# Local attention and two feed-forward layers on one core: scalings on GpSimd, padded V, one copy of the second transpose bank, and a new start

## The chip, the cores and the metric

The kernel runs on one core of a Trainium2 chip. A core has five engines with their own instruction streams: PE (TensorE, matrix products), DVE (VectorE), ACT (ScalarE), POOL (GpSimd) and SP, which here only starts DMA transfers; they wait for each other by semaphores. PE, DVE and ACT reach the eight PSUM banks; POOL works on SBUF only. The metric is the device time of one execution in microseconds (us).

## The reference

Attention with a window and a few global keys, then two feed-forward layers; batch 2, 8 heads, 768 positions, head size 64, all in float32:

```python
scores = scale * np.matmul(q, k.transpose(0, 1, 3, 2))
rel = pos[:, None] - pos[None, :]; is_global = pos[None, :] < 8; is_local = (rel >= 0) & (rel < 96)
keep = is_global | is_local
dist = np.where(is_global & ~is_local, 96.0, np.abs(rel))
bias = -slopes[:, None, None] * dist[None, :, :]
scores = np.where(keep, scores + bias[None], -1e9)
a = np.exp(scores - np.max(scores, axis=-1, keepdims=True))
a = a / (np.sum(a, axis=-1, keepdims=True) + 1e-09)
x = np.matmul(a, v)                # -> 1536 tokens x 512
h = x @ w_in;  g = np.where(h > 0, h, np.exp(np.minimum(h, 0)) - 1);  x = g @ w_out
h = x @ w_in2; g = h / (1 + np.exp(-1.702 * h));                      x = g @ w_out2
```

The weights (512x2048 and 2048x512) come as float64 and are converted on the chip.

## The kernel before

**Attention** goes by rows of 128 queries: 12 rows, each in two units of two head pairs, 24 units `u`. A unit of a row that isn't the first of its batch sees 192 keys for each half of the queries; in a first row (units 0, 1, 12, 13) 64 and 128. A unit does, in this order:
- scores on four 64x64 quarters of the array (L330);
- for each of its four blocks `n` a DVE reduce that adds the distance bias and finds the extreme (L639) and an ACT exponential with its sum (L643). The bias is a product of distances and the head's slope: for first rows made per unit by `slope` (`E<-d,slope`: DVE L245 or ACT L553), for others once in `dist` (`d<-gt,slope`);
- 1e-9 and reciprocal (L646, L649), then four scalings of the weights by the reciprocal (`o_ts`, DVE, L245);
- PE transposes into bank `ta` (L661, L664) and bank `tb` (L668, L670);
- copies of the banks to `pt` (`evac`, L677, ACT or DVE). The keys of the two query halves overlap in `tb`: rows 0 to 63 are needed with V's own block, rows 64 to 127 with the block before it (`va`). They are copied apart to `pt[0:64, 0:256]` and `pt[64:128, 768:1024]`, whose other halves `Band` filled with zeros on POOL (L543, L544), so that a product over all 128 rows is right;
- P times V (L700) on two halves of the array, 64 columns of weights each, and, each second unit, `xh` and `xl`, the two parts of the result for the layers (L716, L719).

A float32 matmul stands as two instructions in the trace. `E` has three buffers, `pt` two.

**The layers** run as products of high and low parts (three matmuls for one): `A` (L432, first product, with its activation, L441 to L450), `B` (L472, second product, L489, L493). Weights are converted by `conv`, eight tiles of 128x512 for a group: DMA to `raw`, a scaled copy to `m` (L399 on ACT or L400 on DVE), L402, L404 and L406 on DVE's integer path, then high part (L233, L234) and low part (L240).

**The order** of all this within the branch `banded` is made by `Plan`, a list scheduler that runs while the program is written: each node has a due time, one or more engines it can go to with a cost for each, and keys that it reads and writes. An engine takes, among the nodes that could start soonest, the one due first; a node with several engines goes where its end, plus `BIAS` (DVE 1.373, ACT 0.264, POOL 0), is soonest. `START` says when each engine is free, `TIMES` the distance of the units' due times, `CONV0` that of the first conversions. If PE would wait early in the kernel, the plan puts fillers on it (L732), products of zeros into a free bank, to keep its clock up.

**The start** (`start`, before the branch): the loads, six warm-up matmuls (L282), distances `rel` on POOL and DVE, the scores of row 0, then from the two integers `n_global` and `n_local` (`n_raw`) on DVE a flag (L288 to L295) that says whether the banded form holds, the scaled window (L296, L297) and `d0`, the distances of a first row (L300, L301, twice each). Every engine loads the flag and branches.

## Time and profile before

| what | us |
|---|---|
| median of 3 runs | 613.66 |
| lowest, highest | 613.49, 614.02 |
| the profiled execution | 613.83 |
| its span, first to last instruction | 612.0 |
| PE busy | 599.4 |
| DVE busy | 403.8 |
| ACT busy | 316.3 |
| POOL busy | 4.6 |

Times in rows are microseconds from the span's start unless marked ns. A busy engine had at least one instruction under way; matmuls overlap, so the pace of a run of them is read from start to start. `PEld` is PE's loading of weights. `PEclk` is the granted clock of PE, 1.00 for 2.4 GHz and 0.50 for 1.2 GHz.

### The profile page before, as it was taken

Reading aid. Unit: us, or ns where it says so; the run is one execution under the profiler, and the core shown is the slowest. Engines: PE = TensorE matmul, PEld = TensorE weight load, DVE = VectorE, ACT = ScalarE, POOL = GpSimd, SP = SyncE. Lnnn points to the kernel's source line nnn. Section 1 sums busy time; section 2 is a strip of 40 time slices with the busy share of each in tenths; the row PEclk is TensorE's granted clock in tenths of the full one; section 3 lists DMA queues with packets and bytes.
Section 4 is the critical chain, followed back from the end, with each engine's and each line's share of the span. In section 5 each row is a group of like instructions: output and inputs, shape, how many; then the busy total and the mean of one; then the engine's idle time right before and its main releaser. Section 6 shows DMA issues by size and latency. Waiting matters only on the chain.

```text
span 612.0 us, 8793 instructions
## 1 busy us (share of the span) xinstructions
PE 599.4 (98%) x3332; PEld 494.3 (81%) x3332; DVE 403.8 (66%) x926; ACT 316.3 (52%) x700; POOL 4.6 (1%) x34
## 2 busy tenths in 40 slices
PE   8988999999999999999999999999999999999996
PEld 5777887788888888888888888888888888888885
DVE  7999898539853994489747973388438853753432
ACT  5999889658552562265456553454214522521320
POOL 3000000000000000000000000000000000000000
PEclk9989999999999999999999999999999999999999
DMA  7755565002220331013201330043002320001012
GB/s 262 256 174 190 191 198 189 29 1 101 92 83 1 103 130 43 1 70 131 77 1 35 103 137 1 1 137 126 13 2 103 104 69 1 35 1 69 18 52 74
DMA packets 16467, 52.04 MB, mean 85 GB/s; under 512 B 1952, under 2 KB 2208, under 8 KB 16416
## 3 DMA queue, kind: packets, MB, share of 16 engines
q1 hardware_dynamic: 16128, 50.73, 24.0%
q10 hardware_dynamic: 288, 0.66, 0.3%
q8 instruction: 28, 0.46, 0.3%
q14 instruction: 23, 0.19, 0.1%
HBM read 48.24 MB, written 3.15 MB: 84 GB/s over the span
## 4 chain that ended last, share of the span: by engine, by line
PE 92%; ACT 3%; DVE 3%; DMA 1%; issue 0%; DVEq 0%; ACTq 0%
PE bank L432 43%; PE bank L472 42%; PE bank L700 3%; PE bank L330 2%; PE bank L664 1%; ACT E L643 1%; ACT pt L677 1%; DVE E L639 1%; DVE E L245 1%; DMA n_raw<-in_ns_dram 1%; PE bank L670 0%; ACT m L399 0%; ACT xh L716 0%; ACT E L553 0%; DVE xl L719 0%
## 5 line engine op out<-in xcount | busy, mean ns | idle before, releaser
L432 PE MATMUL bank<-xh,wbig 128*128 128x512 f32 (+1 forms) x560 | 173.6, 381 | 2.5 <-DVE xl L719 1.8
L432 PEld LDWEIGHTS bank<-xh,wbig 128*128 128x128 f32 x560 | 104.4, 189 | 24.3 <-DVE xl L719 2.6
L432 PE MATMUL bank<-xl,wbig 128*128 128x512 f32 (+1 forms) x280 | 105.8, 378 | 0.0
L472 PE MATMUL bank<-g,wbig 128*128 128x512 f32 (+1 forms) x360 | 81.5, 368 | 0.4 <-DVE xl L719 0.2
L432 PE MATMUL bank<-xh,kT 128*128 128x512 f32 x240 | 77.6, 391 | 0.0
L472 PEld LDWEIGHTS bank<-g,wbig 128*128 128x128 f32 x360 | 62.5, 188 | 12.6 <-issue 1.0
L493 DVE SCALAR_TENSOR_TENSOR acc<-bank,acc 128x512 f32<-128x512 f32 x48 | 33.2, 692 | 50.0 <-PE bank L472 49.6
L448 ACT ACTIVATE e<-bank 128x512 f32<-128x512 f32 x48 | 28.6, 596 | 68.0 <-PE bank L432 67.9
L432 PEld LDWEIGHTS bank<-xl,wbig 128*128 128x128 f32 x280 | 53.0, 189 | 9.5
L472 PE MATMUL bank<-wbig,g 128*128 128x512 f32 (+1 forms) x246 | 59.8, 384 | 0.0
L240 DVE TENSOR_TENSOR g<-gt,g 128x512 fp32r<-128x512 f32 (+1 forms) x70 | 46.4, 663 | 19.8 <-ACT g L233 18.6
L233 ACT ACTIVATE wbig<-m 128x512 fp32r<-128x512 f32 x43 | 27.0, 628 | 60.7 <-PE bank L432 39.8
L233 ACT ACTIVATE g<-gt 128x512 fp32r<-128x512 f32 (+1 forms) x70 | 42.6, 608 | 24.0 <-DVE gt L450 15.0
L450 DVE SCALAR_TENSOR_TENSOR gt<-e,bank 128x512 f32<-128x512 f32 x48 | 32.9, 686 | 31.1 <-ACT e L448 30.7
L432 PEld LDWEIGHTS bank<-xh,kT 128*128 128x128 f32 x240 | 45.0, 188 | 9.9 <-issue 0.6
L472 PEld LDWEIGHTS bank<-wbig,g 128*128 128x128 f32 x246 | 45.4, 188 | 9.1
L445 DVE SCALAR_TENSOR_TENSOR gt<-e,bank 128x512 f32<-128x512 f32 (+1 forms) x52 | 33.3, 644 | 21.1 <-ACT e L443 20.6
L432 PE MATMUL bank<-xl,kT 128*128 128x512 f32 x120 | 46.7, 389 | 0.0
L399 ACT ACTIVATE m<-raw 128x512 f32<-128x512 f32 x56 | 37.2, 664 | 15.0 <-DMA raw<-in_w2i_dram 5.9
L404 DVE SCALAR_TENSOR_TENSOR raw<-raw 128x512 int32<-128x512 int32 x64 | 44.1, 689 | 0.8
L406 DVE SCALAR_TENSOR_TENSOR m<-m,raw 128x512 int32<-128x512 int32 x64 | 44.0, 688 | 0.8
L643 ACT ACTIVATE E<-E,st 128x192 f32<-128x192 f32 (+1 forms) x96 | 41.2, 431 | 3.8 <-DVE st L639 3.7
(122 smaller groups left out, 847.0 us busy)
## 6 DMA issues: line engine op xcount, KB each, us to landing
raw<-in_w1i_dram SPq DMA_DIRECT2D x16, 512.0 KB, 3.3
raw<-in_w1o_dram SPq DMA_DIRECT2D x16, 512.0 KB, 3.3
raw<-in_w2i_dram SPq DMA_DIRECT2D x16, 512.0 KB, 3.2
raw<-in_w2o_dram SPq DMA_DIRECT2D x16, 512.0 KB, 3.3
row<-in_qk_dram SPq DMA_DIRECT2D x8, 768.0 KB, 6.4
v<-in_v_dram SPq DMA_DIRECT2D x12, 256.0 KB, 3.5
va<-in_v_dram SPq DMA_DIRECT2D x10, 256.0 KB, 3.8
out_dram<-acc SPq DMA_DIRECT2D x8, 256.0 KB, 2.0
```

The source lines that it names most:

```text
L233: ("ACT", n / 1200 + (0.05 if psum else 0.09), lambda: nc.scalar.activation(out, in_, AF.Copy)),
L240: return [("DVE", n / 960 + 0.068, lambda: nc.vector.tensor_tensor(out, a, b, ALU.subtract))]
L399: ("ACT", 0.52, lambda: nc.scalar.activation(mf, topf, AF.Copy, scale=sc)),
L404: node(due + 1, [("DVE", 0.6, lambda: V.scalar_tensor_tensor(top, bot, 29, top, ALU.logical_shift_right, ALU.bitwise_or))], [kr], [kr])
L406: node(due + 1.5, [("DVE", 0.6, lambda: V.scalar_tensor_tensor(m, m, 3, top, ALU.logical_shift_left, ALU.bitwise_or))], [km, kr], [km])
L432: nc.tensor.matmul(h(), lhsT=w[:, kk, :], rhs=x[:, kk, :], start=(kk == 0 and j == 0), stop=(kk == KK - 1 and j == 2))
L445: node(due + 1, [("DVE", n / 960 + 0.07, lambda: V.scalar_tensor_tensor(gt, e, -1.0, h(), ALU.add, ALU.max))], [ke, b], [kg], uses=[b])
L448: node(due, [("ACT", n / 1200 + 0.05, lambda: S.activation(e, h(), AF.Tanh, scale=0.851))], [b], [ke], uses=[b])
L450: node(due + 1, [("DVE", n / 960 + 0.07, lambda: V.scalar_tensor_tensor(gt, e, 1.0, h(), ALU.add, ALU.mult))], [ke, b], [kg], uses=[b])
L472: nc.tensor.matmul(o(), lhsT=lhsT, rhs=rhs, start=(f == 0 and j == 0), stop=(f == GF - 1 and j == 2))
L493: node(due, [("DVE", n / 960 + 0.07, lambda: V.scalar_tensor_tensor(acc, o(), sc, acc, ALU.mult, ALU.add))], [b] + ka, ka, uses=[b])
L643: node(at + 0.5, [("ACT", W / 1200 + 0.28, lambda n=n, e=e: nc.scalar.activation(e, e, AF.Exp, bias=st[:, n:n + 1], scale=-1.0, accum_out= ...
```

## The change

- The scalings of the weights by the reciprocal, and the products with the slope, get POOL as a further choice in the plan (`o_scale` in place of `o_ts`).
- `tb` is copied once, whole, to `pt[:, 512:768]`; `pt` loses its zero halves. Instead V is padded: `vz` (V's rows 0 to 63, zeros below) and `vaz` (zeros, and `va`'s rows 64 to 127), made by a POOL copy of 64x512 for each load of V and of `va`. One half of the queries uses `vz` with `va`, the other `v` with `vaz`, so P times V becomes twice as many matmuls of 64 columns instead of 128. In first rows the second transposes take all 128 columns; `E`'s columns 192 to 255 are set to zero at the start.
- At the start: `n_raw` is loaded on ACT's queue instead of SP's, row 0's halves change queues, row 1 comes in one transfer on SP; the flag's chain has one dependent step less (an extra instruction for negative integers moves to the general branch); `d0` is made by two instructions over 192 columns from a copy of the distances (`own`).
- The plan: new start times, due times, first conversions and costs; PE's nodes carry a `mode`, the tiling of the array they use, and a node of another mode counts as 0.1 us later and as due 2 us later; transposes keep the order of the units.

```diff
-CONV0 = (-12.46, 4.78)
+CONV0 = (-12.46, 4.0)
-TIMES = (8.0, 4.0, 3.25)
+TIMES = (7.0, 3.0, 2.6)
-START = dict(PE=5.8, ACT=5.1, DVE=5.9, POOL=5.9, SP=5.6)
+START = dict(PE=5.3, ACT=5.0, DVE=5.2, POOL=6.3, SP=5.0)
-ROW0 = 5.2, 5.8
+ROW0 = 4.9, 5.8
+DRAIN = 0.1
+KEEP = 2.0
+RESERVE = 1000.0
...
+                if e == "PE":
+                    wait = min((x[1] for x in ts if x[0] >= 1e9), default=1e9) + RESERVE
+                    ts = [(1e9 if lst[i].alloc and due > wait else t + DRAIN * (
+                        lst[i].mode != self.mode), due + KEEP * (lst[i].mode != self.mode), i)
+                        for t, due, i in ts]
...
-def o_ts(k, out, in_, s1, s2, op0, op1, n):
-    nc = k.nc
-    return [("DVE", n / 1920 + 0.068, lambda: nc.vector.tensor_scalar(out, in_, s1, s2, op0, op1))]
+def o_scale(k, out, in_, c, n):
+
+    op = lambda e: lambda: e.tensor_scalar(out, in_, c, 1.0, ALU.mult, ALU.mult)
+    return [("DVE", n / 1940 + 0.13, op(k.nc.vector)), ("POOL", n / 760 + 0.268, op(k.nc.gpsimd))]
...
-    nc.sync.dma_start(out=raw, in_=ns.bitcast(I32).partition_broadcast(128))
+    nc.scalar.dma_start(out=raw, in_=ns.bitcast(I32).partition_broadcast(128))
     load()
...
+    for e in k.E:
+        G.memset(e[:, :, QW:256], 0.0)
...
+    for (x, n), at in zip(OWN, (128, 2 * QW - 128)):
+        V.tensor_copy(own[:, x:x + n], rel[:, at:at + n])
...
-    V.scalar_tensor_tensor(neg, lo, 0.0, hi, ALU.is_lt, ALU.add)
-    V.scalar_tensor_tensor(n, neg, float(2.0 ** 32), lo, ALU.mult, ALU.add)
-    k.ng, k.nl = n[:, 0:1], n[:, 1:2]
-    V.scalar_tensor_tensor(a, n, 1.0, lim, ALU.mult, ALU.is_le)
-    V.scalar_tensor_tensor(c, k.nl, 1.0, a[:, 1:2], ALU.is_ge, ALU.mult)
-    V.tensor_tensor(flag, c, a[:, 0:1], ALU.mult)
+    V.scalar_tensor_tensor(k.n, k.f[:, 1:4:2], float(2.0 ** 32), k.f[:, 0:4:2], ALU.mult, ALU.add)
+    k.ng, k.nl = k.n[:, 0:1], k.n[:, 1:2]
+    V.scalar_tensor_tensor(a, k.n, 1.0, lim, ALU.mult, ALU.is_le)
+    for x in range(2):
+        V.scalar_tensor_tensor(c[:, x:x + 1], k.n[:, x:x + 1], float(x), a[:, x:x + 1], ALU.is_ge,
+                               ALU.mult)
+    V.tensor_tensor(flag, c[:, 0:1], c[:, 1:2], ALU.mult)
...
-    for x, n, (d, _) in ((128, 64, OWN[0]), (2 * QW - 128, 128, OWN[1])):
-        at, to = rel[:, x:x + n], k.d0[:, d:d + n]
-        V.scalar_tensor_tensor(w[:, 0:n], at, k.ns, k.big[:, 0:n], ALU.is_ge, ALU.mult)
-        V.scalar_tensor_tensor(to, at, k.ns, w[:, 0:n], ALU.min, ALU.add)
+    V.scalar_tensor_tensor(w, own, k.ns, k.big, ALU.is_ge, ALU.mult)
+    V.scalar_tensor_tensor(k.d0, own, k.ns, w, ALU.min, ALU.add)
...
-        self.pt = [t([128, 1024], F32, f"pt{i}") for i in range(2)]
-        for pt in self.pt:
-            k.nc.gpsimd.memset(pt[64:128, 0:256], 0.0)
-            k.nc.gpsimd.memset(pt[0:64, 768:1024], 0.0)
+        self.pt = [t([128, 768], F32, f"pt{i}") for i in range(2)]
+        self.vz = [t([128, H, D], F32, "vz"), k.d[:, :, QW:256]]
+        self.vaz = [t([128, H, D], F32, "vaz")] * 2
...
+        for kind, z, v, rows in (("v", self.vz[p], self.v[p], slice(0, 64)),
+                                 ("va", self.vaz[p], self.va[p], slice(64, 128))):
+            if kind == "v" or r % NB:
+                node(due + 11, [("POOL", 0.63, lambda z=z, v=v, rows=rows: k.nc.gpsimd.tensor_copy(
+                    z[rows], v[rows]))], [(kind, p)], [self.kz[kind][p]])
...
-            evac(due + 3, pt[:, 256:768], lambda: ta.tile, ta, kp[1], 512)
-            evac(due + 3.3, pt[64:128, 768:1024], lambda: tb.tile[64:128, 0:256], tb, kp[2], 256)
-        evac(due + 3.2, pt[0:64, 0:256], lambda: tb.tile[0:64, 0:256], tb, kp[0], 256)
+            evac(due + 3, pt[:, 0:512], lambda: ta.tile, ta, kp[0], 512)
+        evac(due + 3.2, pt[:, 512:768], lambda: tb.tile[:, 0:256], tb, kp[1], 256)
...
             for j, pr in enumerate(prs):
...
+                for x in range(2):
+                    ws = ((self.v if x else self.vz)[p], (self.vaz if x else self.va)[p])
+                    at = (2 * j + 1, 4 + j) if x else (4 + j, 2 * j)
+                    for own in range(first, 2):
+                        for hd in range(2):
+                            o, c = pr * 128 + 64 * x, 128 * at[1 - own] + 64 * (hd ^ x)
+                            nc.tensor.matmul(
+                                xb.tile[64 * hd:64 * hd + 64, o:o + 64],
+                                lhsT=ws[1 - own][:, 2 * pr + hd, :], rhs=pt[:, c:c + 64],
+                                start=(own == first), stop=(own == 1))
...
-        for r in range(2):
-            load_row(r, (nc.scalar, nc.sync))
+        load_row(0, (nc.sync, nc.scalar))
+        load_row(1)
         load_v(0, k.v[0])
```

## Rows read from the trace of the kernel before

**Rows 1.** Table by stretch: us, busy time (instructions) by engine, clock, DMA.
```profile
8.00:67.00 59.00, 54.30 (x584) 44.47 (x583) 55.65 (x243) 57.04 (x192) 0.36 (x2) 0.97 0.61 211
67.00:606.60 539.60, 539.60 (x2714) 446.36 (x2713) 343.01 (x666) 257.46 (x506) 0.00 (x0) 1.00 0.20 70
```

**Rows 2.** Chain that ended last: start us, us, what.
```profile
6.10 0.16 DVE n_flag L295
6.55 0.30 DVE e L300
...
7.58 0.36 DVE d L301
...
8.45 0.22 DVE E L639
...
145.08 10.88 PE bank L472 x48
```

**Rows 3.** PE's timeline, then L732 by stretch, PE and PEld.
```profile
22.36 1.67 PE L732 MATMUL bank<-q1h 128*128 128x256 f32 x12
...
8.00:14.30 6.30, 3.60 (x22) 3.02 (x22) 1.00 0.87 325
...
8.00:67.00 59.00, 7.32 (x42) 5.73 (x42) 0.97 0.61 211
```

**Rows 4.** PE's waits in 8 to 67 us; table by stretch.
```profile
PE bank L432 <- DVE xl L719: 1.8, 1, 1.8
...
37.70:41.10 3.40, 3.40 (x22) 3.07 (x17) 3.28 (x16) 3.29 (x10) 0.00 (x0) 0.50 0.47 162
```

**Rows 5.** Busy time by stretch of L245 (DVE), then of L553 (ACT).
```profile
8.00:67.00 59.00, 14.70 (x60) 0.97 0.61 211
...
8.00:67.00 59.00, 4.87 (x15) 0.97 0.61 211
```

**Rows 6.** Groups by form, 8 to 67 us: xcount, busy us, mean ns, idle.
```profile
L677 ACT ACTIVATE pt<-bank 64x256 f32<-64x256 f32 x23 | 8.6, 373 | 0.2
...
L677 ACT ACTIVATE pt<-bank 128x512 f32<-128x512 f32 x10 | 5.9, 591 | 0.4 <-PE bank L670 0.3
...
L404 DVE SCALAR_TENSOR_TENSOR raw<-raw 128x512 int32<-128x512 int32 x8 | 5.5, 691 | 0.1
...
L240 DVE TENSOR_TENSOR wbig<-m,wbig 128x512 fp32r<-128x512 f32 x7 | 4.8, 690 | 0.2
...
L402 DVE TENSOR_SCALAR raw<-raw 128x512 int32<-128x512 int32 x8 | 3.4, 427 | 0.3 <-ACT m L399 0.3
```

**Rows 7.** Table by stretch, 40 to 70 us.
```profile
40.00:70.00 30.00, 28.41 (x280) 23.90 (x279) 27.19 (x99) 27.90 (x88) 0.00 (x0) 0.98 0.51 169
```

**Rows 8.** POOL's timeline.
```profile
4.60 0.29 POOL masks.py:199 TENSOR_SCALAR_AFFINE_SELECT ident<-ident 128x128 f32<-128x128 f32 x1
...
7.39 0.30 POOL L544 MEMSET pt<- 64x256 f32 x1
```

**Rows 9.** DVE's timeline: the cast that waits for `n_raw`.
```profile
5.04 0.17 DVE L288 CAST n_f<-n_raw 128x4 f32<-128x4 int32 x1 [1.88 <-DMA n_raw<-in_ns_dram]
```

**Rows 10.** PE's timeline; groups by form from 70.25 to 70.5 us.
```profile
43.45 0.44 PE L700 MATMUL bank<-pt,va 128*64 128x128 f32 x4
...
44.48 0.88 PE L330 MATMUL bank<-row 64*64 64x192 f32 x16
...
L330 PE MATMUL bank<-row 64*64 64x64 f32 x8 | 0.4, 230 | 0.0
```

**Rows 11.** Timelines of DVE and POOL at the start.
```profile
1.70 0.47 DVE L277 TENSOR_SCALAR e<-e,n_off 128x384 f32<-128x384 f32 x1 [0.28 <-POOL e L265]
2.01 0.19 POOL L274 MEMSET slope<- 64x1 f32 x1
2.60 0.56 DVE L279 TENSOR_TENSOR e<-e,gt 128x384 f32<-128x384 f32 x1
2.65 0.09 POOL L274 MEMSET slope<- 64x1 f32 x1
```

More of the change, by code (lines that the diff above doesn't have):

```diff
@@ L66 @@
 class Node:
[L67 removed]
+    __slots__ = ("due", "opts", "npred", "succ", "ready", "alloc", "uses", "spare", "mode")
 ENGINES = ("PE", "ACT", "DVE", "POOL", "SP")
@@ L98, in __init__, with node @@
         self.cand = {e: [] for e in self.avail}
-    def node(self, due, opts, reads=(), writes=(), alloc=None, uses=(), spare=2):
+        self.mode = "full"
+    def node(self, due, opts, reads=(), writes=(), alloc=None, uses=(), spare=2, mode="full"):
         n = Node()
+        n.mode = mode
         alloc = [] if alloc is None else alloc if isinstance(alloc, list) else [alloc]
@@ L206, in place @@
         cost = opt[1]
+        if e == "PE" and self.mode != n.mode:
+            t, self.mode = max(t, self.avail[e] + DRAIN), n.mode
         if e == "PE" and t < WARM:
@@ L608, in unit @@
         pt = self.pt[u % 2]
-        kp = [("pt", u % 2, x) for x in range(3)]
+        kp = [("pt", u % 2, x) for x in range(2)]
         V = nc.vector
@@ L623, in unit @@
             halves = range(2) if whole else (half,)
-            node(due, [("PE", 0.25 + (0.23 if first else 0.335) * len(ps), lambda: scores(
-                k, r, ps, [b.tile for b in own]))], self.keys(r, halves), own, alloc=own, uses=own)
+            node(due, [("PE", (0.22 if first else 0.33) * len(ps), lambda: scores(
+                k, r, ps, [b.tile for b in own]))], self.keys(r, halves), own, alloc=own, uses=own,
+                mode="quarters")
         sc = self.sc[2 * half:2 * half + 2] if whole else self.sc
@@ L632, in unit @@
                     d, kd = e, (kE, n)
-                    self.slope(due + 0.1 * n, e, self.d0[:, OWN[x][0]:OWN[x][0] + W], 2 * pr + x, W,
+                    self.slope(due + 0.1 * n, e, self.d0[:, OWN[x][0]:sum(OWN[x])], 2 * pr + x, W,
                                ["d0"], [(kE, n)])
@@ L692, in pv @@
         def pv():
-            blocks = pt.rearrange("p (a b) -> p a b", b=64)
             for j, pr in enumerate(prs):
-                for own in range(first, 2):
-                    v = self.v[p] if own else self.va[p]
-                    for hd in range(2):
-                        a, b = ((2 * j, 6 + 4 * j) if own else (4 + 4 * j, 12 + 2 * j))
-                        a, b = a + hd, b + 1 - hd
-                        nc.tensor.matmul(
-                            xb.tile[64 * hd:64 * hd + 64, pr * 128:(pr + 1) * 128],
-                            lhsT=v[:, 2 * pr + hd, :], rhs=blocks[:, a:b + 1:b - a, :],
-                            start=(own == first), stop=(own == 1))
-        kv = [("v", p)] + ([] if first else [("va", p)])
-        node(due + 4, [("PE", 0.65 if first else 1.1, pv)], kv + kp, [xb],
-             alloc=xb if half == 0 else None, uses=[xb], spare=0)
+                for x in range(2):
[8 more added lines that the diff above has]
+                                start=(own == first), stop=(own == 1))
+        kv = [y for x in ("v", "va")[:2 - first] for y in ((x, p), self.kz[x][p])]
+        node(due + 4, [("PE", 0.5 if first else 0.95, pv)], kv + kp, [xb],
+             alloc=xb if half == 0 else None, uses=[xb], spare=0, mode="columns")
         if half == 0:
```

61 lines of the change are left out of this document (31 added, 30 removed).

## The prediction

> **What bounds the kernel now.** I read the table of busy time by stretch first, then the chain that ended last, then the groups and single instructions of the stretch that the change touches. By stretch [rows 1] the kernel has three parts. From 67 us to 606.6 us TensorE (PE) is busy without a gap at the full granted clock; after it come 5.4 us, to the span's end, of last sums and stores. From 8 to 67 us PE is busy 54.30 of 59 us, while VectorE (DVE) is busy 55.65 and ScalarE (ACT) 57.04: here these two are the limit. GpSimd (POOL) works 0.36 us in that stretch. The chain [rows 2] says the same: it runs through DVE's start instructions until the first `tensor_tensor_reduce` at 8.45 us, then through DVE and ACT, and later, as in its last row shown, through PE alone. So the kernel ends 5.4 us after PE has done its whole work, and a saving is either time that PE wastes before 67 us, or work of PE itself.
>
> What PE wastes in 8 to 67 us has three terms. It isn't busy for 59 - 54.30 = 4.70 us [rows 1]. It runs 42 filler matmuls (L732), which serve only to keep it busy; twelve in a row took 1.67 us [rows 3], 0.139 us each, so 42 take 5.8 us. And one stretch of 3.40 us ran at a granted clock of 0.50, half speed, after PE had waited 1.8 us for `xl` [rows 4]: 1.7 us lost. The sum is 12.2 us, so PE's own work in the stretch is 59 - 12.2 = 46.8 us. That is all that faster DVE and ACT can give there. Of it, 22 fillers (3.1 us) stand before 14.3 us [rows 3], while the first units pass through their chain; more throughput doesn't remove them.
>
> **The change, part by part.**
>
> *The scalings on POOL.* DVE's scalings (L245) take 14.70 us busy in the stretch, 60 of them; ACT's products with the slope (L553) 4.87 us [rows 5]. The planner now has POOL as a third choice for both, with no bias against it, where DVE's end is counted 1.373 us later; I take it that nearly all go there.
>
> *One copy instead of two.* A unit of a row that isn't first copied `tb` twice, 64x256 each, and now once, 128x256. Each such unit makes one copy of 128x512, and the stretch has 10 of them; at 0.373 us a 64x256 copy [rows 6] this takes 3.7 us from ACT. That a copy over 128 partitions costs as much as one over 64 I take from the 128x512 one, 0.591 us: twice the columns and twice the partitions for 1.6 times the price.
>
> *What this gives.* DVE and ACT held 55.65 + 57.04 = 112.7 us. Less 14.70, 4.87 and 3.7 leaves 89.4 us, 44.7 each if the planner spreads what both can do (weight copies, evacuations), and at today's busy share, 112.7/118 = 95.5%, 46.8 us. PE's own work was 46.8 us too. So after the change all three engines would be near their limit together, and then none is always busy: in 40 to 70 us, where today all three come nearest to that, DVE and ACT were busy 27.19 and 27.90 and PE 28.41 of 30 us [rows 7], 5.3% idle. I take 5.3% of a stage of some 48 us, 2.5 us, and the first 3.1 us of fillers as left: 5.6 us wasted instead of 12.2, a gain of **6.6 us**. Bounds: 0 and 12.2 us.
>
> *POOL's own load.* No row has a POOL multiplication by a column of scalars. The nearest are the 128x128 affine select, 0.29 us, and the 64x256 memset, 0.30 us [rows 8]. For 128x192 I take 0.45 us: half as wide again as the select gives 0.44. From below it is 0.29, from above twice the 0.44, 0.88. 60 of them are 27 us. The zero-padded copies are new work on POOL: one 64x512 for each unit, at most twice that memset; I take 0.55 us, for some 13 units 7 us. 34 us together fits in a stage of 48. At 0.88 us it would be 60 us, but the planner then hands what comes late back to DVE. In the chain of a unit, four scalings of 0.45 us, 1.8 us, stand for four that took 14.70/60 each, 1.0 us, on DVE [rows 5]: 0.8 us later, which three `E` buffers carry while PE has other units and FFN work. With that cover gone it would be 0.8 us once for each unit that PE waits for. A copy of V waits for V's load and has the same cover.
>
> *The start.* The flag's chain has five steps after the cast today, the last of them at 6.10 us [rows 2], 1.06 us after the cast's start at 5.04 us [rows 9]: 0.2 us each. Now it has four, and a fifth that waits for nothing new and costs what it takes to issue, some 0.08 us: -0.12 us. Four instructions make `d0`, 6.55 to 7.93 us, 1.38 us [rows 2]. Two over 192 columns replace them; on the chain a 64-wide one takes 0.30 and a 128-wide one 0.36, so 0.42 each, 0.84 in all: -0.5 us. Both lie on the chain to 8.45 us: **-0.6 us**; bounds 0 and -1.1 (POOL's branch and ACT's slopes may still be what the first unit waits for). At nothing I cost: DVE's two copies into `own`, in its wait for `n_raw` (1.88 us idle [rows 9]), 0.7 us if that were gone; POOL's three memsets of `E`, at most 0.9 us by the 64x256 row, between its last start instruction, over at 4.89 us [rows 8], and the flag at 6.1; the order of the loads (`n_raw` is first on ACT's queue as it was on SP's, row 0's second half is behind it, row 1 is whole on SP, and PE has fillers until it is there). POOL's memsets in the branch grow from 4 x 0.30 to 3 x 0.55 us; POOL starts work some 0.4 us later, and ACT and DVE can make the first slopes until then. Were `n_raw` late, everything in the branch would be late by the same.
>
> *PE's own work.* P times V goes from 16 instructions of 128 columns to 32 of 64 for a unit (8 to 16 in a first row's). The columns are the same. Today the 16 take 1.03 us, from 43.45 to 44.48 [rows 10]. Below, nothing is added; above, each 64-column instruction costs what one of 128 does. No row has 64 columns on half the array, but 8 score instructions of 64 columns started on two quarters within 0.25 us beside four wider ones [rows 10], about 0.06 us for each on its quarter. Sixteen on each half at 0.058 are 0.93 us, against 8 at 0.109, 0.87: +0.06 us for 20 units, **+1.3 us** with the first rows'. Against it the planner now charges 0.1 us for a change of the array's tiling and prefers to stay in one. A P times V of 1.03 us holds 0.87 us of columns, so its two edges cost 0.16; if half a change is saved for each of 24 units, that is **-1.0 us** (bounds 0 and -2). All of this lies where PE never waits, so it counts in full: +0.3 us together.
>
> **The sum.** The profiled execution took 613.83 us, 0.2 above the median of 613.66 and 1.8 above its span. 613.83 - 6.6 - 0.6 + 0.3 = **606.9 us**.
>
> **The rivals.**
>
> *POOL and DVE take turns.* POOL's 64x1 memset of 2.01 us took 0.19 us instead of 0.09 and ended 0.03 us after the DVE `tensor_scalar` beside it, that of 1.70 us [rows 11]. So some DVE instructions hold POOL up. If the weight conversion's instructions do so too, POOL's 34 us and DVE's L402, L404, L406 (like L404) and `wbig` L240 (3.4 + 5.5 + 5.5 + 4.8 = 19.2 us [rows 6]) follow one another: 53 us, at 95.5% 55.7 us, and the stage gives back 3.3 us at most; with waits in the units' chain, 2. The time would be about **611.5 us**. Against it: a memset beside the two-input `tensor_tensor` of 2.60 us took 0.09 us [rows 11], but a memset reads nothing. The Trainium skill ("SBUF — State Buffer", the section on the shared port pair) has this as a rule: an exclusive lock, taken by DVE's two-port modes and, against a POOL instruction that reads, by DVE instructions with two SBUF inputs. By that rule the time is this rival's; by the memset row alone it is the forecast's. The first half of the rule agrees with the 0.19 us; the second half no row here shows.
>
> *All waste goes.* If the new order lets PE fill every gap, first fillers included: 613.83 - 12.2 - 0.6 + 0.3 = **601.3 us**. For it: the load of DVE and ACT falls by a fifth. Against: all three engines meet the same 46.8 us.
>
> *Weight loads bound P times V (slower).* If every one of the 32 instructions, whose weights change each time, takes 0.0545 us of the array as today's 16 do, a unit takes 1.89 instead of 1.03 us: 20 x 0.87 + 4 x 0.44 = 19 us, **625 us**. It outweighs the rest from 0.35 us a unit, that is from 38 ns an instruction against 27 by columns. Against it stands the row of 64-column scores.
>
> *Nothing moves, or the new order stumbles.* If the planner's new due times start units that then wait for POOL, waits move rather than go; PE's wait of 1.8 us and its half-clock stretch are what one such place costs, 3.5 us: two of them cancel the gain, 614 us.
>
> **Chances.** Forecast 0.57 (603 to 609.5); all waste gone 0.11; turns 0.17; slow P times V 0.07; stumbling 0.08. The range 600.5 to 612.5 holds the first two and nearly all of the third, 0.83. A difference under 0.2%, 1.2 us, is about what can't be told from no change. Faster (below 612.4): 0.57 + 0.11 + 0.14 = 0.82 less what the first may miss, 0.81; same: 0.03 of the turns and half the stumbling, 0.08; slower 0.11.
>
> **What would show it.** After: POOL busy 25 to 40 us before 67 us; DVE with few scalings; no second copy of `tb`; at most 5 us of PE idle and some 25 fillers; PE's gapless stretch from about 50 us; the first reduce near 7.8 us; a P times V of 1.0 to 1.15 us. Wrong: POOL scalings far above 0.5 us, DVE's conversion instructions longer than today's 0.69, a P times V above 1.3 us, or half-clock stretches after new waits.

## The result and the profile after

| | before | after |
|---|---|---|
| median, us | 613.82 (4 runs) | 608.63 (4 runs, 608.22 to 609.74) |
| ratio | 1 | 0.9919, 95% interval 0.9902 to 0.9936 |
| profiled execution, us | 613.83 | 608.22 |
| its span, us | 612.0 | 606.3 |

The change made the kernel 5.2 us faster; forecast were 6.8 us, from 613.66 to 606.9 us, with a range of 600.5 to 612.5. The sign, the mechanism and the range held; the terms of the sum didn't come out one by one, and the gain that the start made on DVE didn't reach PE. In the changed kernel `L257` is now the scalings and slope products, `L720` P times V, `L752` the fillers, `L345` the scores, `L618` the copies of V.

The table of busy time by stretch of the changed kernel (us, then busy time and instructions of PE, PEld, DVE, ACT, POOL; granted clock; DMA), to be held against [rows 1], with the first scores' stretch, and the stage cut at 30 us:

```profile
7.60:11.00 3.40, 3.10 (x28) 2.55 (x28) 3.00 (x21) 3.23 (x16) 3.23 (x9) 0.52 0.81 273
...
8.00:30.00 22.00, 21.84 (x335) 18.95 (x336) 19.46 (x98) 20.48 (x80) 14.44 (x29) 0.93 0.80 288
30.00:67.00 37.00, 36.57 (x529) 32.73 (x525) 35.35 (x121) 33.85 (x110) 25.97 (x43) 1.00 0.61 207
...
8.00:67.00 59.00, 58.40 (x857) 51.67 (x857) 54.81 (x218) 54.32 (x189) 40.41 (x71) 0.97 0.68 237
67.00:601.00 534.00, 533.60 (x2819) 443.81 (x2819) 332.91 (x617) 249.46 (x479) 23.17 (x39) 1.00 0.20 68
```

The same cut of the kernel before:

```profile
8.00:30.00 22.00, 21.15 (x254) 17.04 (x253) 20.70 (x111) 21.34 (x80) 0.36 (x2) 1.00 0.79 289
30.00:67.00 37.00, 33.15 (x333) 27.43 (x331) 34.94 (x133) 35.70 (x114) 0.00 (x0) 0.95 0.50 165
```

Two things are to be seen. From 30 to 67 us PE was idle 3.85 us before and 0.43 us after. And POOL is now busy 40.4 of 59 us, while DVE and ACT are hardly less busy than before: they do more of the layers' work in the same stretch.

The fillers, PE and PEld by stretch, against [rows 3]:

```profile
8.00:30.00 22.00, 8.83 (x54) 7.55 (x54) 0.93 0.80 288
8.00:67.00 59.00, 9.33 (x56) 7.85 (x56) 0.97 0.68 237
```

There are 56 fillers instead of 42, and 54 of them stand before 30 us, where the kernel before had 40. The chain that ended last (start us, us, what), against [rows 2], runs through them; its last row here is a whole unit's P times V:

```profile
1.17 6.69 DMA acc<-in_qk_dram
...
7.90 1.13 PE bank L345 x12
9.03 2.00 PE bank L752 x8
11.04 1.52 PE bank L345 x32
12.55 2.94 PE bank L752 x23
...
16.95 1.08 PE bank L720 x32
...
60.19 1.11 PE bank L720 x32
```

It begins with a load, that of row 0's second half, and runs through two trains of fillers, eight at 0.25 us and 23 at 0.128 us, while the first units pass through DVE, ACT and POOL. The first P times V comes later than before, by PE's timelines of the two kernels:

```profile
14.33 0.66 PE L700 MATMUL bank<-pt,v 128*64 128x128 f32 x8
```

```profile
15.33 0.38 PE L685 MATMUL bank<-ident,E 128*128 128x128 f32 x2
...
16.89 0.34 PE L720 MATMUL bank<-pt,vz 128*64 128x64 f32 x4
```

Unit 0's scalings aren't the reason: the last of them ends at 12.82 us, at 12.85 before. What follows them in the order is later: the first transposes stand behind the 23 fillers, at 15.33 instead of 12.64 us, and the first copy of a bank comes at 15.75 instead of 13.49 us. PE's waits in 8 to 67 us, the longest (waited for; us in total, times, longest), in place of that of [rows 4]; two of 0.2 us follow it:

```profile
PE bank L345 <- DMA acc<-in_qk_dram: 2.3, 1, 2.3
```

The 1.8 us for `xl` is gone with the half-clock stretch behind it; one wait of 2.3 us stands at the first scores, and the clock of 0.52 from 7.6 to 11.0 us (first table) follows it, which is half clock for nearly all of it. DMA issues from 0 to 9 us (tile, queue, count, KB, median us to landing) show which transfer it is:

```profile
acc<-in_qk_dram SPq DMA_DIRECT2D x1, 256.0 KB, 4.2
acc<-in_qk_dram ACTq DMA_DIRECT2D x1, 256.0 KB, 6.7
n_raw<-in_ns_dram ACTq DMA_DIRECT2D x1, 2.0 KB, 4.3
```

The two halves of row 0 have 256 KB each: 4.2 us on SP's queue, 6.7 us on ACT's behind `n_raw`. DVE's start, against [rows 2] and [rows 9]:

```profile
5.08 0.39 DVE L305 CAST n_f<-n_raw 128x4 f32<-128x4 int32 x1 [1.55 <-DMA n_raw<-in_ns_dram]
...
6.24 0.16 DVE L312 TENSOR_TENSOR n_flag<-n_c 128x1 int32<-128x1 f32 x1
...
7.17 0.42 DVE L316 SCALAR_TENSOR_TENSOR d<-e,n_scaled,gt 128x192 f32<-128x192 f32 x1
7.97 0.62 DVE L581 SCALAR_TENSOR_TENSOR gt<-e,n_scaled 128x384 f32<-128x384 f32 x1 [0.38 <-DVE d L316]
...
8.92 0.22 DVE L663 CUSTOM_DVE_ANT_0 E<-bank,E 128x64 f32<-128x64 f32 x1
...
9.42 0.29 DVE L663 CUSTOM_DVE_ANT_0 E<-bank,E 128x128 f32<-128x128 f32 x1
```

The last of these is unit 0's fourth reduce. In the kernel before it was:

```profile
9.90 0.28 DVE L639 CUSTOM_DVE_ANT_0 E<-bank,E 128x128 f32<-128x128 f32 x1
```

`d0` is ready at 7.59 us, 0.34 earlier than in [rows 2], but the first reduce starts at 8.92 instead of 8.45: the plan now puts the window step (L581, L583) ahead of it. In the kernel before the same step stood behind the first reduce, from 8.60 us, so the fourth one is 0.48 us earlier than before. Groups by form from 8 to 67 us (xcount, busy us, mean ns, idle before), against [rows 6]:

```profile
L257 POOL TENSOR_SCALAR E<-E,st 128x192 f32<-128x192 f32 x32 | 17.9, 573 | 11.0 <-PE bank L720 4.7 <-DVE st L673 3.5 <-ACT wbig L245 1.5
...
L419 DVE SCALAR_TENSOR_TENSOR raw<-raw 128x512 int32<-128x512 int32 x9 | 6.6, 735 | 0.1
L421 DVE SCALAR_TENSOR_TENSOR m<-m,raw 128x512 int32<-128x512 int32 x8 | 6.4, 794 | 0.1
L698 ACT ACTIVATE pt<-bank 128x256 f32<-128x256 f32 x18 | 6.3, 382 | 1.3 <-PE bank L685 1.3
...
L417 DVE TENSOR_SCALAR raw<-raw 128x512 int32<-128x512 int32 x9 | 4.8, 535 | 0.6 <-ACT m L414 0.6
L618 POOL COPY vaz<-va 64x512 f32<-64x512 f32 x6 | 4.7, 787 | 2.7 <-issue 1.5 <-POOL d L618 0.9
```

A POOL scaling takes 0.573 us on average and a copy of V 0.60 to 0.86 (groups of its three tiles); the whole `tb` copy takes 0.382 us, about what each of its two halves took before (0.373). DVE's L421 and L417, which were L406 and L402, are slower than before: 794 against 687 ns and 535 against 427 ns. Busy time of L257 on DVE and POOL, against [rows 5]:

```profile
8.00:67.00 59.00, 5.96 (x19) 29.48 (x55) 0.97 0.68 237
```

Of DVE's 14.70 us, 5.96 are left, and POOL has 29.48 with what came from ACT.

### The profile page after: what moved, and what is told of

The parts are those of the page before. It is cut to its first block, busy times and chain, and to the rows that moved or that the text cites. A ratio compares the mean times of both kernels' runs of the same rounds, so it can differ in the third digit from the quotient of the medians.

```text
span 606.3 us, 9622 instructions
## 1 busy us (share of the span) xinstructions
PE 596.0 (98%) x3698; PEld 497.9 (82%) x3698; DVE 392.9 (65%) x851; ACT 305.6 (50%) x669; POOL 68.6 (11%) x145
## 4 chain that ended last, share of the span: by engine, by line
PE 95%; POOL 2%; DVE 1%; DMA 1%; issue 0%; ACT 0%; ACTq 0%; POOLq 0%
PE bank L487 43%; PE bank L447 42%; PE bank L720 3%; PE bank L345 3%; PE bank L688 2%; PE bank L752 1%; DMA acc<-in_qk_dram 1%; POOL E L257 1%; PE bank L691 1%; POOL vz L618 0%; POOL vaz L618 0%; DVE raw L419 0%; DVE raw L417 0%; DVE m L421 0%; DVE d L508 0%
## 5 line engine op out<-in xcount | busy, mean ns | idle before, releaser
L487 PE MATMUL bank<-g,wbig 128*128 128x512 f32 (+1 forms) x360 | 80.2, 366 | 0.7 <-DVE wbig L252 0.7
L447 PE MATMUL bank<-xh,kT 128*128 128x512 f32 x240 | 76.3, 389 | 0.0
L508 DVE SCALAR_TENSOR_TENSOR acc<-bank,acc 128x512 f32<-128x512 f32 x48 | 33.2, 692 | 54.0 <-PE bank L487 53.8
L252 DVE TENSOR_TENSOR g<-gt,g 128x512 fp32r<-128x512 f32 (+1 forms) x70 | 46.6, 666 | 20.2 <-ACT g L245 19.0
L245 ACT ACTIVATE wbig<-m 128x512 fp32r<-128x512 f32 x42 | 26.5, 630 | 59.5 <-PE bank L447 37.6
L245 ACT ACTIVATE g<-gt 128x512 fp32r<-128x512 f32 (+1 forms) x70 | 42.7, 610 | 24.9 <-DVE gt L465 15.5
L421 DVE SCALAR_TENSOR_TENSOR m<-m,raw 128x512 int32<-128x512 int32 x64 | 45.1, 705 | 0.8
L419 DVE SCALAR_TENSOR_TENSOR raw<-raw 128x512 int32<-128x512 int32 x64 | 44.5, 695 | 0.8
L252 DVE TENSOR_TENSOR wbig<-m,wbig 128x512 fp32r<-128x512 f32 x44 | 30.1, 689 | 22.9 <-ACT wbig L245 22.2
L257 POOL TENSOR_SCALAR E<-E,st 128x192 f32<-128x192 f32 (+1 forms) x74 | 41.9, 581 | 23.9 <-DVE st L673 9.5
```

The source lines that it names most:

```text
L245: ("ACT", n / 1200 + (0.05 if psum else 0.09), lambda: nc.scalar.activation(out, in_, AF.Copy)),
L252: return [("DVE", n / 960 + 0.068, lambda: nc.vector.tensor_tensor(out, a, b, ALU.subtract))]
L257: op = lambda e: lambda: e.tensor_scalar(out, in_, c, 1.0, ALU.mult, ALU.mult)
L419: node(due + 1, [("DVE", 0.6, lambda: V.scalar_tensor_tensor(top, bot, 29, top, ALU.logical_shift_right, ALU.bitwise_or))], [kr], [kr])
L421: node(due + 1.5, [("DVE", 0.6, lambda: V.scalar_tensor_tensor(m, m, 3, top, ALU.logical_shift_left, ALU.bitwise_or))], [km, kr], [km])
L447: nc.tensor.matmul(h(), lhsT=w[:, kk, :], rhs=x[:, kk, :], start=(kk == 0 and j == 0), stop=(kk == KK - 1 and j == 2))
```

## The experiments

The table sums up every run. The columns from "idle" on are worked out from PE's starts in the trace of the profiled execution, from 5 us to the last matmul. The time from one start to the next counts as the matmul's own up to its columns' time at the granted clock plus 0.12 us; what goes beyond that is idle. "Fillers" has their number and own time. "Half clock" is half of the own time of the other matmuls that ran at half clock, so what the clock cost them; "attention" and "layers" are their own time less that. "After" and "before" are the two kernels shown. The first two columns are of all runs, the others of one execution each.

| kernel | us | ratio to before (95% interval) | idle | fillers | half clock | attention | layers |
|---|---|---|---|---|---|---|---|
| before | 613.8 | | 8.6 | 42, 6.6 | 3.2 | 53.5 | 529.5 |
| after | 608.6 | 0.9919 (0.9902 to 0.9936) | 4.9 | 56, 8.4 | 0.6 | 54.6 | 527.4 |
| e1_load | 607.3 | 0.9898 (0.9884 to 0.9913) | 2.9 | 56, 8.4 | 1.4 | 54.6 | 527.4 |
| e5_n_raw_sp | 607.2 | 0.9891 (0.9876 to 0.9907) | 2.7 | 56, 8.4 | 1.5 | 54.5 | 527.4 |
| e8_half_fill | 607.5 | 0.9897 (0.9882 to 0.9912) | 5.6 | 28, 4.7 | 2.0 | 55.2 | 527.3 |
| e10_nraw_slope | 610.6 | 0.9948 (0.9935 to 0.9961) | 6.5 | 50, 6.9 | 0.0 | 55.9 | 528.0 |
| e2_no_pool | 614.5 | 1.0022 (1.0010 to 1.0035) | 6.3 | 72, 11.2 | 1.0 | 54.3 | 528.7 |
| e4_before_pool | 609.5 | 0.9944 (0.9931 to 0.9957) | 8.4 | 38, 5.7 | 1.2 | 54.0 | 527.7 |
| e7_before_copy | 614.9 | 1.0012 (1.0003 to 1.0021) | 6.7 | 46, 7.1 | 2.0 | 55.6 | 529.4 |
| e3_old_copy | 616.8 | 1.0050 (1.0037 to 1.0063) | 9.8 | 53, 8.4 | 3.5 | 53.9 | 528.6 |
| e6_old_plan | 612.8 | 0.9989 (0.9980 to 0.9998) | 6.3 | 59, 9.2 | 0.7 | 54.7 | 529.2 |
| e11_no_drain | 612.6 | 0.9976 (0.9967 to 0.9984) | 6.2 | 62, 9.2 | 2.0 | 53.8 | 528.7 |
| e12_old_due | 610.8 | 0.9955 (0.9944 to 0.9967) | 6.2 | 60, 9.3 | 0.5 | 54.2 | 528.3 |
| e9_memset | 608.0 | 0.9903 (0.9886 to 0.9920) | 3.8 | 56, 8.4 | 0.8 | 54.2 | 527.4 |

The clock at the start needs a second look. The traces hold records of the granted clock only from a first one on: from 4.31 us in the changed kernel, from 10.38 in the kernel before, 10.61 in `e1_load`, 11.04 in `e5_n_raw_sp`, 4.35 in `e10_nraw_slope`. Where there is none, the tables by stretch print 1.00. PE's timelines of the kernel before, of `e5_n_raw_sp` and of `e10_nraw_slope` show the same 32 score matmuls:

```profile
8.88 2.24 PE L330 MATMUL bank<-acc 64*64 64x192 f32 x32
```

```profile
9.72 2.15 PE L345 MATMUL bank<-acc 64*64 64x192 f32 x32
```

```profile
7.99 1.53 PE L345 MATMUL bank<-acc 64*64 64x192 f32 x32
```

In the first two, four of them start every 0.32 us until the first record and every 0.16 us behind it; in the third every 0.16 us from the beginning. So I count the time before the first record as half clock. The kernel before, too, ran at half clock until 10.38 us, and its 1.00 in [rows 3] and above says nothing of that time.

**The start: the loads' order.** Theory: the new order of loads costs time. First, all loads' queues as before, in the changed kernel:

```diff
-    nc.scalar.dma_start(out=raw, in_=ns.bitcast(I32).partition_broadcast(128))
+    nc.sync.dma_start(out=raw, in_=ns.bitcast(I32).partition_broadcast(128))
...
-        load_row(0, (nc.sync, nc.scalar))
-        load_row(1)
+        for r in range(2):
+            load_row(r, (nc.scalar, nc.sync))
```

> The changed kernel with the loads' queues of before: n_raw first on SP, the halves of rows 0 and 1 spread over ACT and SP. Theory S (the start is where the gain is short: row 0's second half lands 1.0 us later than before, PE idles, goes to half clock and the first units come later): PE's second set of scores at 6.9 us instead of 7.9, no half-clock stretch before 15 us, and 1.0 to 2.5 us less than the changed kernel, 606.1 to 607.6 us (ratio to before 0.9875 to 0.990). Rival H (the first units wait for DVE's distances and the branch anyway, so the load is hidden): within 0.6 us of the changed kernel's 608.6.

607.33 us, 1.3 us under the changed kernel. The second scores start at 6.54 instead of 7.90 us, and the first P times V at 15.95 instead of 16.89. The half-clock stretch isn't gone, though: PE runs at half clock until 10.61 us, 11.14 in the changed kernel. Then the first line of that diff alone (`e5_n_raw_sp`):

> The changed kernel with n_raw first on SP's queue again, row 0's halves and row 1 as changed. Theory N (row 0's second half is late because it stands behind n_raw, 128 tiny pieces, on ACT's queue): the second set of scores starts at 6.6 to 7.0 us instead of 7.9, no half-clock stretch, about 607.3 us as with all the queues of before. Rival W (it is late because row 1, 768 KB in one transfer on SP, shares the DMA engines with it from 1.2 us on): second scores at 7.6 us or later, 608.2 to 609 us.

607.15 us, the fastest version of all. Its chain that ended last begins:

```profile
1.18 4.57 DMA acc<-in_qk_dram
```

Row 0's half on ACT's queue takes 4.57 us when `n_raw` isn't ahead of it, 6.69 when it is. So `n_raw`'s place on that queue is the cause, and row 1 in one transfer isn't. On SP's queue `n_raw` is ahead of row 0's other half, and this one lands after 4.6 instead of 4.2 us. By the table the two versions save 2.0 to 2.2 us of idle and lose 0.8 to 0.9 us of that to half clock, of which the changed kernel's execution has less; the profiled executions are 0.9 to 1.0 us apart, the medians 1.3 to 1.5.

**The start: are the fillers in the way?** `e1_load` with every second filler left out:

```diff
-            self.fill(self.k.bank[free[1]])
+            self.nfill = getattr(self, "nfill", 0) + 1
+            if self.nfill % 2:
+                self.fill(self.k.bank[free[1]])
```

> The changed kernel with the loads' queues of before (607.33 us) and every second filler matmul left out, all else in the same order. Theory F (PE comes late to 23 fillers in a row, which then stand in front of the first transposes): the first transposes at 13.0 to 13.6 us instead of 14.4, 605.8 to 606.8 us. Rival G (without the fillers PE's clock is halved for a stretch, or the next wait comes instead): 607 to 609 us.

607.46 us against 607.33, no gain: theory F's early transposes came (12.72 and 13.36 us), its time didn't. PE's timeline (start us, us, what, idle before and its releaser), then a line of ACT's:

```profile
13.36 0.33 PE L687 MATMUL bank<-ident,E 128*128 128x128 f32 x1 [0.30 <-POOL E L259]
...
14.81 0.69 PE L687 MATMUL bank<-ident,E 128*128 128x128 f32 x2 [0.91 <-DVE E L259]
...
15.88 0.34 PE L722 MATMUL bank<-pt,vz 128*64 128x64 f32 x4
```

```profile
14.84 1.35 ACT L700 ACTIVATE pt<-bank 128x256 f32<-128x256 f32 x4
```

The transposes that the fillers stood ahead of now wait for scalings of `E`, ACT makes the first copies only behind the exponentials of the next units, and the first P times V comes 0.07 us earlier than in `e1_load` (15.95). Here the fillers fill a wait; they don't make it. In the changed kernel they do in part: there ACT waited 1.08 us for the transposes behind them, in `e1_load` 0.30 us, since the late load had delayed both trains.

**The start: POOL in the first unit's chain.** `e5_n_raw_sp` with the slope products kept on DVE and ACT:

```diff
-        self.plan.node(due, o_scale(k, out, in_, c, w) + [
+        self.plan.node(due, o_scale(k, out, in_, c, w)[:1] + [
```

> The changed kernel with the load of n_raw first on SP's queue again, and the products with the slope kept on DVE and ACT (POOL has only the scalings by the reciprocal and the copies of V). Theory U (unit 0 is late because POOL makes three d products and a copy before its scalings): its scalings end earlier, the first P times V starts near 15.2 us instead of 16.2, there are 6 to 10 fillers fewer before 30 us, and the time is 0.5 to 1 us under that of the changed kernel with n_raw on SP, 606.2 to 606.7 us. Rival B (DVE and ACT are then the fuller engines and give the same time back in the stage): 607 to 609 us, with more PE idle between 14 and 50 us.

Neither theory came out. The first P times V does start earlier, at 14.84 us instead of 16.22, and there are 50 fillers, but not for theory U's reason: unit 0's scalings end at 13.21 us, in `e5_n_raw_sp` at 12.34. It is the order that differs: ACT copies unit 0's banks from 14.14 us, there from 15.08. The time, 610.61 us, is above rival B's range too, in B's direction. By the table, against `e5_n_raw_sp`, 1.5 us of fillers and 1.5 us of half clock saved, 3.8 us of idle, 1.4 us of attention and 0.6 us of the layers' matmuls added; PE's waits in 5 to 67 us are now for POOL's scalings (1.9 us) and for ACT's copies (1.6 us). An earlier start of the first unit is worth nothing if the throughput behind it falls.

**POOL.** The changed kernel without the choice of POOL for scalings and slope products:

```diff
-    return [("DVE", n / 1940 + 0.13, op(k.nc.vector)), ("POOL", n / 760 + 0.268, op(k.nc.gpsimd))]
+    return [("DVE", n / 1940 + 0.13, op(k.nc.vector))]
```

> The changed kernel without POOL as a choice for the scalings and slope products (POOL keeps the padded copies). Theory P (most of the gain is DVE's relief by POOL): DVE gets 15 us back before 67 us, PE waits and fillers there come back, 611.5 to 613.5 us. Rival C (the single copy and the plan's new due times and tiling order carry the gain, and POOL's slow scalings and the shared SBUF ports give most of theirs back): 608 to 610 us.

614.48 us, above both ranges: without POOL the rest of the change is no gain at all. And POOL alone, put into the kernel before (the cut lines bring in `o_scale` and set POOL's start time to 6.0):

```diff
...
-        self.plan.node(due, o_ts(k, out, in_, c, 1.0, ALU.mult, ALU.mult, w) + [
-            ("ACT", w / 1200 + 0.1, lambda: nc.scalar.activation(out, in_, AF.Copy, scale=c))],
+        self.plan.node(due, o_scale(k, out, in_, c, w) + [
+            ("ACT", w / 1200 + 0.19, lambda: nc.scalar.activation(out, in_, AF.Copy, scale=c))],
...
-            node(due + 2.3, o_ts(k, e, e, st[:, 12 + n:13 + n], 1.0, ALU.mult, ALU.mult, Ws[x]),
+            node(due + 2.3, o_scale(k, e, e, st[:, 12 + n:13 + n], Ws[x]),
```

> The kernel before with POOL as a choice for the scalings and slope products alone, with the costs of the change; due times, copies, loads and start as before. Theory P: a third or more of PE's 12 us of waste before 67 us goes, 608 to 610.5 us. Rival C: 612 to 614 us. POOL's 192-wide scaling lasts 0.55 to 0.6 us on average as in the changed kernel, and L402, L404 and L406 are longer than before by some 0.05 to 0.1 us where POOL works beside them.

609.53 us, 4.3 of the 5.2 us. Its table by stretch, its longest wait of PE in 8 to 75 us, and L404 of the kernel before, which is L405 here:

```profile
8.00:67.00 59.00, 53.90 (x622) 44.46 (x622) 52.25 (x213) 55.73 (x191) 35.53 (x65) 1.00 0.69 242
```

```profile
PE bank L701 <- ACT pt L678: 4.1, 4, 1.9
```

```profile
L405 DVE SCALAR_TENSOR_TENSOR raw<-raw 128x512 int32<-128x512 int32 x9 | 6.2, 684 | 0.0
```

ACT is now the fullest engine, and P times V waits for its copies of the banks. The conversions of two inputs (L405, and L407 with 683 ns) aren't longer than before, against what I had expected, although most of them have POOL scalings beside them.

**The single copy.** Put alone into the kernel before (`vz`, `vaz`, one copy of `tb`, 64-column P times V, the memsets of `E`; the diff is that part of the change's):

> The kernel before with the single copy, the padded V on POOL and P times V of 64 columns alone; scalings on DVE, due times, loads and start as before. ACT loses 3.7 us before 67 us, DVE nothing, PE gains 0.06 us a unit. Theory P: 612 to 614 us. Rival C (the copy carries as much as POOL's scalings, as the changed kernel without it is 8 us slower than with it): 608 to 610.5 us.

614.86 us: ACT falls from 57.04 to 53.16 us busy in 8 to 67 us, and DVE, at 57.51, is now the fullest engine. By the table, in an execution of 613.30 us, idle and half clock fall by 3.1 us, while attention rises by 2.2 and fillers by 0.5: P times V alone takes 2.0 us more by its starts. By these numbers ACT's relief does arrive at PE, and the price of the 64-column P times V takes most of it. And the same part undone in the changed kernel:

```diff
...
-            evac(due + 3, pt[:, 0:512], lambda: ta.tile, ta, kp[0], 512)
-        evac(due + 3.2, pt[:, 512:768], lambda: tb.tile[:, 0:256], tb, kp[1], 256)
+            evac(due + 3, pt[:, 256:768], lambda: ta.tile, ta, kp[1], 512)
+            evac(due + 3.3, pt[64:128, 768:1024], lambda: tb.tile[64:128, 0:256], tb, kp[2], 256)
+        evac(due + 3.2, pt[0:64, 0:256], lambda: tb.tile[0:64, 0:256], tb, kp[0], 256)
...
```

> The changed kernel with the two copies of the second transposes, pt's zero halves and P times V of 128 columns as before; no padded V, so POOL has no copies. ACT gets 3.7 us back before 67 us, PE's P times V loses 0.06 us a unit. Theory P (POOL's scalings carry the gain, the copy little): 607.5 to 609.5 us. Rival C (the single copy carries much of it): 610 to 612 us.

616.78 us, slower than the kernel before and far above both ranges:

```profile
8.00:67.00 59.00, 55.53 (x585) 45.27 (x585) 48.63 (x198) 51.79 (x178) 34.76 (x60) 0.97 0.63 211
```

No engine is full in this stage: DVE has 48.63 us, less than in any other version, and ACT 51.79. Of the 8.2 us against the changed kernel 4.9 are idle of PE and 2.9 half clock: its first record of the clock is at 13.94 us, and after the waits for a copy and two scalings around 35 to 37 us it falls to half again from 37.84 to 41.25. PE waits 1.1 us for scalings and 1.4 us for copies in all. Units stumble over each other here: two copies a unit, in an order of tight due times, hold the banks longer. That is the prediction's last rival, in a version without the single copy. Why the banks should be held so long is argued, not shown: no run separates the tiles and banks involved.

**The plan.** The changed kernel with due times, first conversions and tiling price of before:

```diff
-CONV0 = (-12.46, 4.0)
+CONV0 = (-12.46, 4.78)
...
-TIMES = (7.0, 3.0, 2.6)
+TIMES = (8.0, 4.0, 3.25)
...
-DRAIN = 0.1
-KEEP = 2.0
+DRAIN = 0.0
+KEEP = 0.0
```

> The changed kernel with the due times of before (TIMES, CONV0) and no price for a change of tiling (DRAIN and KEEP 0). Theory P: POOL's relief acts under any due times, 608.5 to 611 us, with PE's waste before 67 us some 2 us more. Rival D (the new due times are what carries the gain beyond the 4.3 us of POOL alone): 611 to 613 us. A P times V with its neighbours loses about 0.1 us a change of tiling more often; if that matters, PE's work after 67 us is 1 to 2 us more.

612.84 us, as rival D has it. This version has POOL, the single copy and the new start under the old due times and price, and is 3.3 us slower than POOL alone (`e4_before_pool`). The two halves of the plan apart, first `DRAIN` and `KEEP` at 0 alone, then `CONV0` and `TIMES` of before alone:

> The changed kernel with the price for a change of the array's tiling taken out (DRAIN and KEEP zero), due times as in the change. With both the due times of before and no price it had taken 612.8 us, 4.2 us more. Theory G (the price is worth about what the prediction gave it, 1 us, since only PE's edges hang on it): 609.2 to 610.2 us, PE's attention work 1 to 2 us more and waits little changed. Rival H (the price carries the order, and without it waits return): 611 to 613 us, with more idle and fillers.

> The changed kernel with the due times of the units and the first conversions of before, the price for a change of tiling as in the change. Theory T (the tighter due times let the units use what POOL gives; with the old ones PE fills and waits): 610.5 to 612 us, fillers 55 to 65, PE idle 5 to 6 us. Rival K (due times don't matter beside the price): 608.3 to 609.2 us. The two losses, of this run and of the one without the price, need not add up to the 4.2 us of both.

612.58 and 610.75 us: 4.0 and 2.1 us lost, together no more than 4.2. Rival H holds for the price, theory T for the due times. By the table the version without the price has 2.2 us more of idle and fillers, among them one wait of 1.5 us of a transpose for DVE, 1.3 us more of the layers' matmuls and 1.4 us more of half clock, which lasted until 13.59 us; attention at full clock isn't longer. So about half of what the price gives comes through the order. Whether the half clock belongs to the version or to this execution, no run shows.

**Do POOL and DVE take turns?** The changed kernel with POOL's products as memsets to zero of the same tiles; these multiplications are left out:

```diff
-    op = lambda e: lambda: e.tensor_scalar(out, in_, c, 1.0, ALU.mult, ALU.mult)
+    op = lambda e: lambda: (e.tensor_scalar(out, in_, c, 1.0, ALU.mult, ALU.mult) if e is k.nc.vector else e.memset(out, 0.0))
```

> The changed kernel in which each product that the plan gives to POOL (scalings of E by the reciprocal, and products with the slope) is a memset of the same tile to zero: those multiplications are left out, POOL then writes as much but reads nothing. Theory R (POOL's reads and DVE's instructions with two SBUF inputs take turns; in the changed kernel the conversion's L421 took 794 ns on average from 8 to 67 us, at most 1105, against 687 before, L419 735 against 691): without POOL's reads L421 and L419 return to 0.68 to 0.70 us on average with no instruction far above, and POOL's memsets stay at 0.2 to 0.35 us. Rival W (POOL's writes are enough, or the stretch comes from other traffic in SBUF): L421 and L419 stay above 0.73 us and memsets reach 0.5 us or more beside them. L417, which has one input and ran at 427 ns before and 535 after, tells the rest: near 0.43 it was held by reads alone too, above 0.5 by anything that POOL does.

The groups by form from 8 to 67 us:

```profile
L419 DVE SCALAR_TENSOR_TENSOR raw<-raw 128x512 int32<-128x512 int32 x9 | 6.6, 734 | 0.1
L421 DVE SCALAR_TENSOR_TENSOR m<-m,raw 128x512 int32<-128x512 int32 x9 | 6.2, 684 | 0.1
...
L417 DVE TENSOR_SCALAR raw<-raw 128x512 int32<-128x512 int32 x9 | 4.3, 479 | 0.1
...
L257 POOL MEMSET E<- 128x192 f32 x32 | 8.0, 270 | 10.3 <-ACT E L667 9.6 <-PE bank L688 0.2 <-PE bank L720 0.2
```

L421 is back at 684 ns; L419's mean isn't. Its single instructions tell why. DVE's timeline:

```profile
28.34 0.68 DVE L419 SCALAR_TENSOR_TENSOR raw<-raw 128x512 int32<-128x512 int32 x1
...
45.74 0.82 DVE L419 SCALAR_TENSOR_TENSOR raw<-raw 128x512 int32<-128x512 int32 x1
...
48.92 0.69 DVE L419 SCALAR_TENSOR_TENSOR raw<-raw 128x512 int32<-128x512 int32 x1
```

POOL's at the same times:

```profile
28.25 0.98 POOL L257 MEMSET E<- 128x192 f32 x4
...
45.28 0.73 POOL L618 COPY d<-v 64x512 f32<-64x512 f32 x1 [2.50 <-DMA v<-in_v_dram]
...
49.06 1.02 POOL L618 COPY vaz<-va 64x512 f32<-64x512 f32 x1 [2.03 <-issue]
```

The L419 of 0.82 us started while POOL read V; that of 0.68 us ran beside memsets from end to end. That of 0.69 us started 0.14 us ahead of a copy, and here the copy is the one that got longer, 1.02 instead of the 0.60 us that an undisturbed one takes. It is so throughout: of L419 and L421, the two stretched instructions (0.82 and 0.98 us) both began beside a copy of V that had been under way for 0.27 us or more; four that had a copy begin behind them took 0.68 to 0.69 us, and these copies 0.73 to 1.02; three that had memsets beside them for 0.5 us or more, and no copy, took 0.68 to 0.69 us. So theory R holds, with one thing added: the instruction that comes second is the one stretched. That fits the conversions of `e4_before_pool`, which stayed at 0.68 us: there POOL's products beside them took up to 1.35 us. Where the two start within some 0.3 us of each other, the recorded starts don't tell which came second. The Trainium skill ("SBUF — State Buffer", "Who interferes with whom") has it as a lock, which a DVE instruction with two SBUF inputs takes against a POOL instruction that reads SBUF; the trace agrees, with these numbers. L417, with one input and a mean of 479 ns, lies between the two values that I had set and decides nothing by itself; its longest, 0.83 us, lay beside two copies. But the price in time is small: with POOL busy 21.7 instead of 40.4 us the kernel takes 607.95 us, 0.7 less than the changed kernel, and their intervals overlap.

## Why the prediction came out as it did

The profiled execution fell by 5.6 us, 613.83 to 608.22, and the start of PE's last matmul by 5.7, 606.67 to 600.98. The prediction's ledger for PE, filled in by the rule of the table of runs (us, before and after):

| stretch, us | idle | fillers | half clock |
|---|---|---|---|
| 5 to 8 | 0.8, 2.4 | 0.3, 0 | 0.9, 0.1 |
| 8 to 30 | 1.8, 0.7 | 5.9, 8.1 | 0.7, 0.5 |
| 30 to 67 | 5.3, 1.4 | 0.4, 0.3 | 1.6, 0 |
| from 67 | 0.7, 0.4 | 0, 0 | 0, 0 |

In sum -4.4 us: idle -3.7, fillers +1.8, half clock -2.6; by stretch +0.5, +0.9, -5.5 and -0.3. PE's own work at full clock gives -1.0, and the rest is that the first scores start sooner.

- **The stage, -6.6 forecast: the mechanism held, the term was mis-sized where it was split.** From 8 to 67 us the waste fell by 4.6 us, with opposite signs on the two sides of 30 us. After 30 us three quarters of it went: PE not busy 3.85 to 0.43 us, no half clock, two fillers in either kernel. The 5.3% idle that I took over from a stretch in which all engines were full didn't come: PE's timeline shows no wait between 29.7 and 57.4 us. Before 30 us it grew: 25 fillers forecast, 54 found. That the first units' chain would stay as long as it was is the step that failed: the first P times V starts at 16.89 instead of 14.33 us. The prediction also read 1.00 for the clock before 10.38 us, where PE ran at half clock; 0.7 us of scores and some 0.4 of fillers behind 8 us were waste that it didn't see.
- **The start, -0.6 forecast: it came on DVE and got no further.** Unit 0's fourth reduce is 0.48 us earlier. Then its scalings, one on DVE and three on POOL, take 1.26 instead of 0.80 us, the slower chain that the prediction had named without a price in the sum, and end when they did before. On PE the load order, costed at nothing, costs 0.9 to 1.5 us (`e1_load`, `e5_n_raw_sp`). The flag wasn't earlier (6.24 against 6.10 us): a step fewer, but the cast took 0.22 us longer. `d0` came 0.34 us earlier, its two instructions 0.42 each as forecast.
- **PE's own work, +0.3 forecast: about -1.0 at full clock.** P times V did what was forecast: 1.08 to 1.11 us against 1.03 [rows 10] for a unit, +1.3 us in sum; with weights that change each time 64 columns hold their pace, so the slow rival falls. The layers gave back 2.1 us and the transposes 0.3, where the tiling price was to give 1.0. The price isn't all of that: without it the layers lose 1.3 us (`e11_no_drain`), and `e4_before_pool`, which never had it, has nearly the same 527.7.
- **POOL's load.** 34 us forecast, 40.4 found with memsets. The sum had 60 products, without ACT's 15; POOL took 55, and DVE kept 19. A scaling takes 0.42 to 0.43 us where nothing holds it, as forecast, and up to 1.03 us beside a conversion or a subtraction (L252) of DVE, 0.573 us on average, inside the bounds. It is no bound of the stage: with half of it the time is nearly the same (`e9_memset`).
- **The rival "POOL and DVE take turns"** has a real mechanism and the wrong price. L419 and L421 lose 9 x 0.044 + 8 x 0.107 = 1.3 us in the stage and L417 another 1.0, not 19.2 us one after another with POOL's whole load: most POOL instructions lie where DVE does something else.
- **Where the gain comes from.** POOL alone gives 4.3 us (`e4_before_pool`), and without it nothing is left (`e2_no_pool`). Then ACT's copies are the next wait. The single copy pays only together with POOL and the new plan: alone it gives nothing (`e7_before_copy`), with POOL under the due times and the tiling price of before the time is 612.8 us, and without it the rest takes 616.8. So these act as one. My sum of loads, 112.7 less 23.3 us, treats them as terms that add up; the runs show they don't.

That the profiled execution came within 1.3 us of the forecast is in part luck: the 2.0 us that the stage fell short and 0.7 to 0.8 us at the start stand against 1.3 us of PE's own work and 0.3 us behind 67 us that weren't forecast.

Open: how much of the 8 us that two copies cost under the new due times is the order and how much the half clock that came with it; and what decides when PE first gets the full clock, at 4.31 us in one version and at 13.94 in another.

## What to carry to other kernels

Relief of one engine is worth what the next wait lets through: put each part alone into the old kernel and take it alone out of the new one before believing a sum of loads. In a list-scheduled kernel a changed cost or due time is a change of the whole order, so follow the first unit's chain step by step through the new order, the loads' queues included. Where a tiny transfer of many pieces stands is worth a run of its own: ahead of one half of row 0 it cost 2.1 us, ahead of the other half, on the other queue, 0.4. And a table's clock of 1.00 is to be held against the pace from start to start before a half-clock stretch is ruled out.
